# Scaling the features instead of the weights, with a new job order and a new block schedule, in a fused transformer block

## The chip, the cores and the metric

The kernel runs on one core of one Trainium2 chip. The metric is device microseconds (us) for one execution. A comparison is made with runs of the kernel before that were timed on the same chip in the same rounds; its medians in the four sets of rounds after the prediction lie between 392.31 and 392.51 us, so times of different sets may be compared to about 0.2 us. The span of a profile is about 2 us shorter than the time of the same execution, so profiles are compared with profiles and times with times.

The engines are called TensorE (PE; its weight loads PEld), VectorE (DVE), ScalarE (ACT), GpSimd (POOL) and SyncE (SP, which issues nearly all transfers).

## The reference

The reference is one block with modulation from a vector c: layer norm, attention with softmax feature maps (32 heads of 18 columns), a gated residual, layer norm, a two-layer network with ReLU, and a second gated residual.

```python
mod = (_silu(c) @ w_mod).reshape(c.shape[0], 6, 1, -1)      # sa, ca, ga, sb, cb, gb
h = _layernorm(x, axis=-1) * (1 + ca) + sa
x = x + ga * _A_ref(h, A_wqkv, A_w_phi, A_wo)
h = _layernorm(x, axis=-1) * (1 + cb) + sb
x = x + gb * _B_ref(h, B_w1, B_w2)
# _A_ref: q, k, v = h @ wqkv;  phi(u) = [softmax(u @ w_phi), softmax(-u @ w_phi)] per head
#         kv = phi(k)^T v;  o = phi(q) kv / (phi(q) z);  return o @ wo
```

There are 2048 rows of 576 columns (16 row tiles of 128) and 4608 hidden columns, all in bf16.

## The kernel before

It has two parts. The **front** does the attention statistics of all tiles, the queries, and the first two tiles up to the second norm. It is a list of jobs, written in a fixed order (ORDER); each engine gets its instructions in that order. A number after a job is a tile, and a number after a colon is a pair of PSUM banks. Then eight **feed-forward blocks** of two tiles follow. Each also carries, in hooks, the attention output, projection and norm of the two tiles that come next.

```python
ORDER = """
Z11 sx sd rp sc FK ca Z2 fs0 fsr frr fra2 sh frd4 fra0 fra1 bn1 fs3 bn0 fs1 Z1 fra3 shc sa0 wsd2 KR:0 fsd4 fs2
...
kv12 vE14 rK15 kv13 V15:1 qs1 pA15 gar pM15 kv14 Q2:2 vE15 qp1 kv15 eQ2 Q3:0 tp0 wo4 qt1 kz Q4:1 eQ3 wo2 sq2
...
"""
# Z: filler matmuls on zeros   sc, sh: products that give the modulation's scale and shift   FK: fold of w_k with w_phi
# fs, fsr, fsd, wsd, FQs: scaled weight copies   fra, frr, frd: unscaled ones (wfold)   KR, VR, QR: row corrections
# K, V, Q: projections of a tile   pM: GpSimd part of the key softmax   kv: K^T V product
# qs, qp, qt: query softmax (VectorE, GpSimd) and its DMA transpose   gar: the gate row's load   wo: wo *= gate row (GpSimd)
# ... cut ...
    def mods(w, outs, width, bank, idle=None):
        o = PS[:, bank, :] if isinstance(bank, int) else bank[:, 0, :]
        for k, wm in enumerate(w):
            for ci in range(NC):
                if idle is not None:
                    spin(1, idle)                       # one filler matmul of 512 columns
                for ck in range(NC):
                    pe.matmul(...)                      # one column each
# ... cut ...
        # the query softmax of a later tile q, as the hooks below do it:
        #   q_fin(q): q_sm on VectorE, q_pool on GpSimd, q_turn: DMA transpose; then q_in(q + NL), a reload, if there is one
        def in_l1(g, u):
            if (g, u) in ((0, -1), (0, 1)): ...         # the two query softmaxes
            if (g, u) in ((1, 2), (2, 1)):              # attention output of the two tiles, then its DMA transpose
                num_mm(t, pr); num_o(t, pr); turn_dma(oT[:, t % 2], o_sb[:, t % 2, :])
        def in_l2(pos):
            if pos in (1, 4): ...                       # projection wo_mm (5 chunks of 128 rows), residual, statistics
            if pos in (2, 6): ...                       # second norm, then its DMA transpose into h2
            if pos == 12:                               # scale and shift h2 for the next block
                for ci in range(NC):
                    dve.tensor_scalar(out=hb[:, ci, :], in0=hb[:, ci, :], scalar1=..., scalar2=..., op0=ALU.mult, op1=ALU.add)
```

The softmax here doesn't subtract the row's maximum and nothing guards it: scores larger than these inputs give would overflow.

Of the kernel before, what the change touches and what calls it, by code (L numbers as in the profile page):

```python
# [43 lines left out]
Z11 sx sd rp sc FK ca Z2 fs0 fsr frr fra2 sh frd4 fra0 fra1 bn1 fs3 bn0 fs1 Z1 fra3 shc sa0 wsd2 KR:0 fsd4 fs2  # L44
sp0 bn2 T0:2 VR:1 KRh bn3 Tc0 Ka0:2 KRd sa2 wsd1 sp2 VRh Kb0 wsd0 Ka1:0 wsd4 eKa0 VRd Kb1 wsd3 T2:1 eKa1 sK0
V0:2 Tc2 sK1 FQ3:0 rK0 K3:1 FQra3 pA0 FQs3 pM0 vE0 eK3 K2:0 bn4 bn5 rK1 kv0 eK2 FQ1:2 pA1 V1:1 sK3 pM1 FQra1
m2:0 vE1 rK3 sa4 pA3 sK2 FQs1 kv1 sp4 V2:1 m2c pM3 bn7 rK2 T4:2 V3:0 bn6 Tc4 pA2 vE2 pM2 sa6 K4:2 vE3 K5:1
bn10 eK4 sp6 bn9 T6:0 kv2 Tc6 kv3 eK5 sK4 ga:2 K7:0 gac sK5 rK4 K6:1 eK7 pA4 pM4 bn8 V4:2 eK6 sK7 gb:0 sa8
V5:1 vE4 wl0 rK7 sp8 rK5 sK6 pA7 T8:2 gbc kv4 pA5 Tc8 FQ2:0 pM5 K8:2 vE5 rK6 FQrd2 K9:1 bn11 eK8 w2a2 pA6 pM6
bn14 kv5 sa10 V6:2 FQs2 sK8 eK9 sp10 wl1 V7:0 pM7 vE6 rK8 sK9 T10:1 V8:2 Tc10 pA8 vE7 pM8 K10:1 rK9 vE8 w2a0  # L50
kv6 bn12 eK10 FQ0:0 pA9 FQ4:2 kv7 pM9 FQrd0 kv8 FQrd4 V9:1 FQs0 w2b0 bn13 FQs4 QR:0 vE9 K11:2 QRh sa12 QRe
sK10 sp12 kv9 eK11 V10:1 bn15 QRd wl4 rK10 T12:0 V11:2 sK11 Tc12 pA10 sa14 pM10 K13:0 gbw vE10 rK11 wl2 Q0:1
pA11 eK13 sp14 vE11 pM11 kv10 eQ0 T14:2 sK13 K12:0 w2a1 Tc14 qs0 kv11 rK13 K14:1 eK12 pA13 pM13 V13:2 eK14
sK12 wl3 K15:0 qp0 vE13 rK12 sK14 V12:1 eK15 pA12 pM12 qt0 Q1:2 vE12 rK14 sK15 gbr V14:0 pA14 eQ1 gaw pM14
kv12 vE14 rK15 kv13 V15:1 qs1 pA15 gar pM15 kv14 Q2:2 vE15 qp1 kv15 eQ2 Q3:0 tp0 wo4 qt1 kz Q4:1 eQ3 wo2 sq2
tp2 Q5:2 eQ4 sq3 tp1 wo3 nu0:3 eQ5 Q6:0 sq4 nO0 wo0 qi2 Q7:1 eQ6 wo1 sq5 ot0:2 w2b1 eQ7 nu1:3 Q8:0 nO1 oc0
Q9:1 eQ8 W0:3 eQ9 sq7 lb0 ot1:2 sq8 Q10:0 oc1 sq6 lr0 W1:1 ap0 eQ10 sq9 lb1 xc0 ht0:2 sq10 Q11:0 ha0 hd0 lr1
Q12:3 eQ11 ap1 Q13:2 qi3 xc1 eQ12 sq11 ht1:0 Q14:1 hd1 ha1 sq12 eQ13 Q15:3 qi4 eQ14 sq13 eQ15 sq14 sq15
# [3 lines left out]
def tile_block(ctx, tc, a, out):  # L62
# [42 lines left out]
    wv_raw = carve(R1, 12760, (NC, D))  # L105
    wfold = carve(R1, 15640, (NC, D))
# [96 lines left out]
    load(sp, flat(wsc), "wsc")  # L203
    load(sp, flat(wkT), "wkT")
    load_xT(0)
    load(sp, flat(wsh), "wsh")
    load_x(0, 2)
    load(sp, flat(wv_raw), "wv")
    load_x(2, 2)
    load_xT(1)  # L210
    load_x(4, 2)
    load(sp, epsr[:], "epsr")
    load(sp, flat(wqT), "wqT")
    load_xT(2)
# [28 lines left out]
    def mods(w, outs, width, bank, idle=None):  # L243

        o = PS[:, bank, :] if isinstance(bank, int) else bank[:, 0, :]
        for k, wm in enumerate(w):
            for ci in range(NC):
                if idle is not None:
                    spin(1, idle)
                for ck in range(NC):  # L250
                    pe.matmul(o[0:width, k * NC + ci:k * NC + ci + 1], lhsT=wm[0:R, ck, ci * width:(ci + 1) * width],
                              rhs=siluc[0:R, ck:ck + 1], start=(ck == 0), stop=(ck == NC - 1))
# [152 lines left out]
    def wo_mm(t, pr, add_x):  # L405
        for k in range(2):
            if add_x:
                pe.matmul(pr[:, k, 0:HD], lhsT=ident[:, 0:P], rhs=x_sb[:, t, k * HD:(k + 1) * HD], start=True, stop=False)
            for ci in range(NC):
                pe.matmul(pr[:, k, 0:HD], lhsT=oT[:, t % 2, ci, :], rhs=wo_sb[:, ci, k * HD:(k + 1) * HD],  # L410
                          start=(ci == 0 and not add_x), stop=(ci == NC - 1))
# [5 lines left out]
    def ln2_apply(t, src):  # L417
# [4 lines left out]
        if src is None:  # L422
            cols(xn[:, t % 2, 0:D], x_sb[:, t, :])
            cols(xn[:, t % 2, D:640], x_sb[:, t, 512:D])
        else:
            cols(v2(xn[:, t % 2, 0:D]), src[:, :, 0:HD])
            cols(xn[:, t % 2, D:640], src[:, 1, 224:HD])
# [15 lines left out]
    def f_scaled_d(dst, ck):  # L443
        dve.tensor_scalar(out=dst[0:R, ck, 0:G5], in0=PS[0:R, ck, 0:G5], scalar1=ca1[0:R, ck:ck + 1], scalar2=None, op0=ALU.mult)

    def f_scaled(dst, ck):
        act.activation(out=dst[0:R, ck, 0:G5], in_=PS[0:R, ck, 0:G5], func=ACT.Copy, scale=ca1[0:R, ck:ck + 1])

    def f_raw(eng, ck):
        if eng is act:  # L450
            act.activation(out=wfold[0:R, ck, 0:G5], in_=PS[0:R, ck, 0:G5], func=ACT.Copy)
        else:
            eng.tensor_copy(out=wfold[0:R, ck, 0:G5], in_=PS[0:R, ck, 0:G5])
# [12 lines left out]
    SS = RS[:, 0:6 * HD].bitcast(FP32).rearrange("p (a f) -> p a f", f=HD)  # L466
    X, Y, Z = 6, 4, 7
# [8 lines left out]
    def rows_h(pr):  # L476
        act.activation(out=v2(tmpr[X0:NX, :]), in_=pr[X0:NX, :, 0:HD], func=ACT.Copy)

    def rows_d(pr, dst):

        dve.scalar_tensor_tensor(out=v2(dst[X0:NX, 4, :]), in0=v2(tmpr[X0:NX, :]), scalar=mk[X0:NX, :],
                                 in1=pr[X0:NX, :, 0:HD], op0=ALU.mult, op1=ALU.add)
# [24 lines left out]

    def raw_copy(eng, o, i):
# [4 lines left out]

    def wv_scale(ck, eng):
        o, i, f = wv[0:R, ck, :], wv_raw[0:R, ck, :], ca1[0:R, ck:ck + 1]
        if eng is act:
            act.activation(out=o, in_=i, func=ACT.Copy, scale=f)
        else:
            eng.tensor_scalar(out=o, in0=i, scalar1=f, scalar2=None, op0=ALU.mult)

    def ln2_bn(i, pr):
        for hf in range(2):
            dve.bn_stats(out=st[:, i, hf, :], in_=pr[:, hf, 0:HD])
        dve.bn_aggr(out=mv[:, 1, i, :], in_=st[:, i])
# [71 lines left out]
    def k_minus(t):  # L596
# [7 lines left out]
    ROWS = {"K": wfold, "V": wv_raw, "Q": wfold}  # L604
    ROWD = {"K": wk, "V": wv, "Q": wq}
# [6 lines left out]
        "sc": lambda: mods([wsc], None, R, 7, idle=6),  # L612
        "sh": lambda: mods([wsh], None, R, 7, idle=6),
        "shc": lambda: dve.tensor_copy(m98[0:R, :, X0 + 3], PS[0:R, 7, 0:NC]),
        "FK": lambda: fold_all(wkT),
        "fs": lambda c: f_scaled(wk, c), "fsd": lambda c: f_scaled_d(wk, c),
        "frd": lambda c: f_raw(dve, c), "fra": lambda c: f_raw(act, c),
        "fsr": lambda: dve.tensor_tensor(out=wk[0:R, :, G5:D], in0=last,
                                         in1=ca1[0:R, :].unsqueeze(2).to_broadcast([R, NC, FW]), op=ALU.mult),
        "frr": lambda: dve.tensor_copy(out=wfold[0:R, :, G5:D], in_=last),  # L620
        "rp": lambda: pool.tensor_copy(rep[0:R], siluc[0:R, :].unsqueeze(2).to_broadcast([R, NC, 32])),
        "wsd": lambda c: wv_scale(c, dve), "wsa": lambda c: wv_scale(c, act), "wsp": lambda c: wv_scale(c, pool),
# [8 lines left out]
        "FQs": lambda c: act.activation(out=v2(wq[0:R, c, :]), in_=at["FQ", c][0:R, :, 0:HD], func=ACT.Copy, scale=ca1[0:R, c:c + 1]),  # L631
        "FQrd": lambda c: raw_copy(dve, v2(wfold[0:R, c, :]), at["FQ", c][0:R, :, 0:HD]),
        "FQra": lambda c: raw_copy(act, v2(wfold[0:R, c, :]), at["FQ", c][0:R, :, 0:HD]),
        "Q": lambda t: proj(at["Q", t], t, wq), "eQ": lambda t: exps(t, at["Q", t], EQ[:, SLOT[t], :]),
        "sq": q_out, "qi": q_in, "qs": q_sm, "qp": q_pool, "qt": q_turn,
        "m2": lambda: mods([wsb, wcb], None, P, at["m2", None]), "m2c": lambda: mod2_e(at["m2", None]),
# [6 lines left out]
        "W": lambda i: wo_mm(i, at["W", i], True), "lb": lambda i: ln2_bn(i, at["W", i]), "lr": ln2_rs,  # L643
        "xc": lambda i: act.activation(out=v2(x_sb[:, i, :]), in_=at["W", i][:, :, 0:HD], func=ACT.Copy),
        "ap": lambda i: ln2_apply(i, at["W", i]),
# [4 lines left out]
    for w in "KV":  # L650
        JOBS[w + "R"] = lambda w=w: rows_mm(ROWS[w], at[w + "R", None])
        JOBS[w + "Rh"] = lambda w=w: rows_h(at[w + "R", None])
        JOBS[w + "Rd"] = lambda w=w: rows_d(at[w + "R", None], ROWD[w])
    for i, w in enumerate("Q"):
# [3 lines left out]
        JOBS[w + "Rd"] = lambda w=w, i=i: quarter_rows(i, ROWD[w])  # L658
# [42 lines left out]
    def l1(b, hooks):  # L701
        hb = h2[:, b % 2]
        for g in range(3):
# [5 lines left out]
            for u in range(3):  # L709
                l1_rest(js[u], u, hb)  # L710
            for u in range(3):
# [19 lines left out]
    def l2(b, hooks):  # L731
# [31 lines left out]
        fin(t + 1, 1, Z, 2)  # L763
        prod(X, A22, T4, al)
# [7 lines left out]
        rows, z = slice(t * P, (t + 1) * P), yt[:, 1, :]  # L772
        sp.dma_start(outf[rows, 0:HD], x_sb[:, t, 0:HD])
        pool.tensor_tensor(out=z, in0=SS[:, 1, :], in1=gb_row[:, HD:D], op=ALU.mult)
        pool.tensor_tensor(out=z, in0=z, in1=x_sb[:, t, HD:D], op=ALU.add)
        prod(Z, A12, B22, al)
        dve.tensor_tensor(out=yt[:, 0, :], in0=PS[:, Z, 0:HD], in1=gb_row[:, HD:D], op=ALU.mult)
        dve.tensor_tensor(out=x_sb[:, t, HD:D], in0=yt[:, 0, :], in1=z, op=ALU.add)
        sp.dma_start(outf[rows, HD:D], x_sb[:, t, HD:D])

    NB = NT // 2
    for b in range(NB):
# [3 lines left out]
        def in_l1(g, u):  # L786
            if not more:
                return
            if (g, u) in ((0, -1), (0, 1)):
                q = t0 + max(u, 0)  # L790
                q_fin(q)
                if q + NL < NT:
                    q_in(q + NL)
            if (g, u) in ((1, 2), (2, 1)):
# [133 lines left out]
```

## Time and profile before

| what | kernel before | from |
|---|---|---|
| time | 393.02 us, median of 3 | runs before the prediction |
| span of the profile | 390.7 us | page |
| first feed-forward matmul | 93.52 us | timeline of TensorE |
| blocks 0 to 6 | 37.05 us each | starts of their first matmuls |
| last block, to the end | 37.83 us | same |
| TensorE busy | 98% | page |

The front and the blocks are read apart, because a change in one says nothing of the other. TensorE is the bound, so each question is whether something takes matmuls away or makes TensorE wait. The lines that show this stand in the prediction.

### The profile page before, as it was taken

How to read it: one execution, taken by the hardware profiler on the slowest of the kernel's cores; microseconds unless marked ns; L12 is line 12 of the kernel's file. 1: busy time of each engine (PE TensorE's matmuls, PEld its weight loads, DVE VectorE, ACT ScalarE, POOL GpSimd, SP SyncE). 2: the span in 40 equal slices, each digit the busy share in tenths (PEclk: the TensorE clock that was granted, in tenths of full speed). 3: DMA queues.
4: the chain of work that ended last, by engine and by line, in shares of the span. 5: the costliest groups of instructions: out<-in, count | busy, mean ns of one | idle time of the engine just before them, and what ended most of it. 6: DMA issues, size and time to landing. Idle time of an engine off the chain costs nothing.

```text
span 390.7 us, 8908 instructions
## 1 busy us (share of the span) xinstructions
PE 383.8 (98%) x3693; PEld 311.7 (80%) x3693; DVE 244.3 (63%) x452; ACT 157.9 (40%) x360; POOL 142.3 (36%) x199
## 2 busy tenths in 40 slices
PE   8999999999999999999999999999999999999995
PEld 4778888878887888788888878887888788878874
DVE  0889998854879746573755567458555664653221
ACT  1798779699531233124213510531143123312510
POOL 2155858741101510740164045306510641072045
PEclk9999999999999999999999999999999999999999
DMA  7999739795732151125313311450143124010001
GB/s 291 418 420 403 274 133 354 178 306 161 189 65 35 47 121 20 35 61 109 35 27 83 80 35 32 107 65 19 47 93 35 24 69 51 18 34 33 3 0 32
DMA packets 49515, 44.36 MB, mean 114 GB/s; under 512 B 39361, under 2 KB 42050, under 8 KB 48706
## 3 DMA queue, kind: packets, MB, share of 16 engines
q1 hardware_dynamic: 49186, 43.59, 39.6%
q8 instruction: 29, 0.48, 0.5%
q10 hardware_dynamic: 288, 0.19, 0.2%
q14 instruction: 12, 0.10, 0.1%
HBM read 27.97 MB, written 6.49 MB: 88 GB/s over the span
## 4 chain that ended last, share of the span: by engine, by line
PE 86%; POOL 6%; ACT 2%; DVE 2%; DMA 2%; issue 1%; SPq 0%; POOLq 0%; DVEq 0%; ACTq 0%
PE PS L683 33%; PE PS L742 29%; PE PS L274 9%; PE PS L410 5%; PE PS L690 5%; POOL wo_sb L637 2%; PE PS L235 2%; PE PS L391 1%; ACT RT L279 1%; POOL RH L754 1%; DMA gatd<-gt 1%; PE PS L324 1%; POOL RT L291 1%; DMA ga_row<-gatd 1%; DVE st L240 1%
## 5 line engine op out<-in xcount | busy, mean ns | idle before, releaser
L683 PE MATMUL PS<-h,R 128*128 128x256 bf16 x1152 | 133.5, 273 | 0.0
L683 PEld LDWEIGHTS <-R 128*128 128x128 bf16 x1152 | 109.8, 98 | 17.5 <-issue 5.1
L742 PEld LDWEIGHTS <-RH 128*128 128x128 f16 x864 | 84.5, 98 | 21.8
L728 POOL TENSOR_TENSOR yt<-yt,gb_row 128x288 f32<-128x288 f32 x23 | 16.8, 731 | 167.0 <-DVE yt L727 167.0
L742 PE MATMUL PS<-R,RH 128*128 128x288 bf16 (+1 forms) x576 | 75.6, 286 | 0.0
L697 ACT ACTIVATE RH<-PS 128x256 f16<-128x256 f32 x72 | 27.7, 384 | 114.0 <-PE PS L690 107.4
L699 DVE SCALAR_TENSOR_TENSOR RH<-PS,RH 128x256 f16<-128x256 f32 x72 | 30.1, 419 | 68.2 <-ACT RH L697 68.2
L279 ACT ACTIVATE RT<-PS,rs 128x576 bf16<-128x576 f32 x64 | 43.0, 750 | 7.5 <-PE PS L274 7.1
L698 ACT ACTIVATE RH<-PS 128x512 f16<-128x512 f32 x72 | 42.9, 595 | 7.8 <-PE PS L683 6.5
L746 ACT ACTIVATE RS<-PS 128x288 f32<-128x288 f32 x24 | 9.9, 411 | 75.9 <-PE PS L742 75.9
L742 PE MATMUL PS<-RT,RH 128*128 128x288 f16 x288 | 37.9, 286 | 0.0
L274 PE MATMUL PS<-RH,R 116*128 116x288 bf16 x240 | 31.8, 286 | 0.5 <-ACT RH L631 0.5
L754 POOL TENSOR_TENSOR RH<-RH,RT 128x2304 f16<-128x2304 f16 x7 | 31.8, 4548 | 0.0
L274 PE MATMUL PS<-RH,RT 116*128 116x288 bf16 x240 | 31.7, 286 | 0.0
L274 PEld LDWEIGHTS <-R 116*128 116x128 bf16 x240 | 22.9, 98 | 6.4 <-issue 0.7
L274 PEld LDWEIGHTS <-RT 116*128 116x128 bf16 x240 | 22.7, 98 | 5.5
L420 DVE TENSOR_SCALAR xn<-x_sb,mv,rs 128x576 bf16<-128x576 bf16 (+1 forms) x28 | 22.4, 842 | 7.3 <-ACT rs L415 7.3
L729 POOL TENSOR_TENSOR x_sb<-yt,x_sb 128x288 bf16<-128x288 f32 x31 | 22.8, 737 | 5.9 <-DVE yt L725 4.1
L240 DVE BATCH_NORM_STATS2 st<-x_sb 128x6 f32<-128x288 bf16 x60 | 24.2, 445 | 0.5
L410 PE MATMUL PS<-wo_sb,oT 128*128 128x288 bf16 x160 | 22.6, 286 | 0.2 <-POOL wo_sb L637 0.2
L284 DVE TENSOR_REDUCE Rk<-RT 128x64 f32<-128x1152 bf16 x16 | 21.2, 1332 | 1.4 <-ACT RT L279 1.4
L284 DVE TENSOR_REDUCE Rq<-RT 128x64 f32<-128x1152 bf16 x16 | 21.5, 1342 | 0.0
(115 smaller groups left out, 414.2 us busy)
## 6 DMA issues: line engine op xcount, KB each, us to landing
R<-in_w1a_dram SPq DMA_DIRECT2D x4, 1152.0 KB
eqd<-RT SPq DMA_DIRECT2D x14, 288.0 KB, 5.8
RT<-eqd SPq DMA_DIRECT2D x14, 288.0 KB, 2.7
R<-in_w2a_dram SPq DMA_DIRECT2D x3, 864.0 KB, 10.4
R<-in_w2b_dram SPq DMA_DIRECT2D x2, 1296.0 KB, 10.9
out_dram<-x_sb SPq DMA_DIRECT2D x15, 144.0 KB, 3.3
RT<-in_xT_dram SPq DMA_DIRECT2D x2, 640.0 KB
x_sb<-in_xk_dram SPq DMA_DIRECT2D x3, 288.0 KB
```

The source lines that it names most:

```text
L240: dve.bn_stats(out=s[:, hf, :], in_=x_sb[:, t, hf * HD:(hf + 1) * HD])
L274: pe.matmul(pr[:, k, 0:HD], lhsT=xt(t, ck), rhs=w[0:R, ck, k * HD:(k + 1) * HD], start=(ck == 0), stop=(ck == NC - 1))
L279: act.activation(out=E.rearrange("p (b h s e) -> p b h s e", b=2, s=2, e=DH)[:, :, :, s, :], in_=pr[:, :, 0:HD].rearrange("p b (h e) -> p ...
L284: dve.tensor_reduce(out=Rr, in_=E.rearrange("p (c e) -> p c e", e=DH), axis=AXX, op=ALU.add)
L410: pe.matmul(pr[:, k, 0:HD], lhsT=oT[:, t % 2, ci, :], rhs=wo_sb[:, ci, k * HD:(k + 1) * HD], start=(ci == 0 and not add_x), stop=(ci == NC ...
L683: pe.matmul(PS[:, 2 * u + hf, n * 256:n * 256 + 256], lhsT=w1a[:, ci, jj * P:(jj + 1) * P], rhs=hb[:, ci, :], start=(n == 0 and ci == 0), ...
L697: act.activation(out=A11[:, j, :], in_=lo[:, :, 0, :], func=ACT.Relu)
L698: act.activation(out=A2[:, j, :, :], in_=PS[:, 2 * u + 1, :].rearrange("p (n s f) -> p n s f", n=2, s=2), func=ACT.Relu)
L699: dve.scalar_tensor_tensor(out=U3[:, j, :], in0=lo[:, :, 1, :], scalar=0.0, in1=A11[:, j, :], op0=ALU.max, op1=ALU.subtract)
L729: pool.tensor_tensor(out=x_sb[:, t, c], in0=y, in1=x_sb[:, t, c], op=ALU.add)
L742: pe.matmul(PS[:, bank, 0:HD], lhsT=am[:, j, :], rhs=bm[:, j, :], start=first and j == 0, stop=(j % 9 == 8), skip_group_check=True)
L754: pool.tensor_tensor(out=A12, in0=A12, in1=U2, op=ALU.subtract)
```

## The change

The intent has five parts: scale the transposed features once and keep one copy of each weight; add the first two residuals on VectorE instead of by identity matmuls; do the half-filled fifth chunk of the output projection as two 64-row matmuls that run beside each other; split the last product in two; and take a new order for the front, searched under the assumption that all loads behind the first eight arrive later. Cut to its core:

```diff
-Z11 sx sd rp sc FK ca Z2 fs0 fsr frr fra2 sh frd4 fra0 fra1 bn1 ...
+Z11 sx sd rp sc bn1 Z2 bn0 FK ca sa0 sp0 fra0 frd4 sh fra1 frr fra2 xd0 T0:0 fra3 Z2 shc Tc0 Ka0:2 ...
 ... cut: the rest of the order; in it
+... QRe QRd V15:1 rK14 sK15 pA14 gar V12:2 pM14 vE14 rK15 Q0:0 vE12 pA15 wo1 vE15 kv12
+eQ0 Q1:2 pM15 Q2:1 qs0 eQ1 wo4 kv13 eQ2 kv14 qs1 kv15 qp0 Q3:0 sq2 tp0 Q4:2 qp1 ...
-    load_x(0, 2)                        # was behind wkT, xT0, wsh
+    load_x(0, 2)                        # now third
-                if idle is not None:
-                    spin(1, idle)
-        "sc": lambda: mods([wsc], None, R, 7, idle=6),
-        "sh": lambda: mods([wsh], None, R, 7, idle=6),
+        "sc": lambda: mods([wsc], R, 7),
+        "sh": lambda: mods([wsh], R, 7),
+    def x_scale(t, eng): ...             # xT of two tiles times (1 + ca); on VectorE, ScalarE or GpSimd
-            if add_x: pe.matmul(pr[:, k, 0:HD], lhsT=ident[:, 0:P], rhs=x_sb[...], start=True, stop=False)
+    def add_res(t, pr): dve.tensor_tensor(out=x, in0=x, in1=pr[:, :, 0:HD], op=ALU.add)
+    def wo_rest(t, pr):                  # fifth chunk: 64 rows at 0 and the same 64 rows at 64, one half of the columns each
+        for k in range(2): pe.matmul(pr[:, k, 0:HD], lhsT=oT[b0:b0 + 64, t % 2, 4, :], rhs=wo_sb[b0:b0 + 64, 4, ...], ...)
         def in_l1(g, u):
+            if b < 2:
+                ...                       # as before, and
+                if b and (g, u) == (1, 0): q_next(t0 + 2)
+                return
+            if (g, u) in ((0, 0), (0, 2)): attend(t0 + u // 2)
+            if g and u == "rest": wo_rest(t0 + g - 1, pair(3))
+            if g and u == 0: wo_full(t, pair(3)); add_res(t, pair(3)); bn(1, t)
+            if (g, u) == (1, 2): norm2(b, t0)
         def in_l2(pos):
 ... cut
+            if pos == (6 if b < 2 else 1): norm2(b, t0 + 1)
+            if b > 1 and pos in (4, 9) or b == 1 and pos == 9: q_next(t0 + 2 + pos // 9)
```

## The prediction

> **What bounds the kernel now.** I read the page's parts 1 and 2 first, then the table of stretches, then the chain in order of time, then TensorE's waits, last the timeline of the first 26 us and of the last 26.
>
> ```profile
> span 390.7 us, 8908 instructions
> PE 383.8 (98%) x3693; PEld 311.7 (80%) x3693; DVE 244.3 (63%) x452; ACT 157.9 (40%) x360; POOL 142.3 (36%) x199
> PE   8999999999999999999999999999999999999995
> ```
>
> TensorE is busy in every slice but the first and the last. Ends of matmuls are modelled, so I checked this with its waits. These are all there are before the feed-forward part begins at 93.68 us (us in total, times, longest):
>
> ```profile
> PE PS L235 <- POOL eps_t L227: 1.3, 1, 1.3
> PE PS L268 <- DVE RS L614: 0.7, 1, 0.7
> PE PS L274 <- ACT RH L631: 0.5, 1, 0.5
> PE PS L577 <- DVE RH L481: 0.3, 1, 0.3
> PE PS L410 <- POOL wo_sb L637: 0.2, 1, 0.2
> ```
>
> After the first 14 us only 1.0 us of waiting is left. So the time is matmul count times spacing, plus the start, plus the tail. The chain from 93.68 us on gives the spacing (start, length, what; the first of eight feed-forward blocks):
>
> ```profile
> 93.68 3.06 PE PS L683 x28
> 96.74 0.76 PE PS L690 x12
> ...
> 113.95 1.23 PE PS L410 x10
> ```
>
> 28 matmuls in 3.06 us: 109 ns for 256 columns. Ten L410 matmuls (288 columns, the output projection of one row tile) in 1.23 us: 123 ns each. Twelve L690 matmuls, which use only 64 rows of the array each, in 0.76 us: 127 ns a pair, little more than one full matmul. Blocks start at 93.68, 130.73, 167.78 and so on: 37.05 us each, seven times. VectorE is busy 22 of these 37 us, so it has room there. It has less in the front (length, PE, PEld, DVE, ACT, POOL busy with counts, clock, DMA share, GB/s):
>
> ```profile
> 0.00:13.25 13.25, 11.95 (x99) 7.40 (x99) 3.57 (x12) 5.24 (x9) 2.22 (x11) 1.00 0.84 323
> 13.25:93.68 80.43, 78.74 (x869) 64.21 (x869) 68.89 (x121) 65.98 (x152) 45.28 (x97) 1.00 0.82 292
> ```
>
> VectorE 68.9 and ScalarE 66.0 of 80.4 us: not the bound, but close behind.
>
> **What the Trainium skill says.** (1) "TensorEngine Tiling (Array Packing)", Key Properties: tiles of different rows can load and multiply in parallel, and changing the tiling mode drains the array. The trace agrees with the first: 127 ns a pair at L690 against 109 ns for one full matmul at L683. The 20 ns over may be the mode change; the trace doesn't separate it. (2) "TensorE: Matmul & The Clock Gate", What's actually happening: the array starts at half rate until about 3.4 us of activity. The trace agrees: the first 12 filler matmuls took 5.30 us (0.44 each), later ones stand about 0.22 us apart. So fillers keep the array awake, and cost nothing while data is awaited. (3) "SBUF — State Buffer", SBUF: two separate sides: VectorE with two SBUF inputs and GpSimd hold one port pair exclusively. The change gives GpSimd three long multiplications; the trace of before has none like them in the front, so it doesn't tell.
>
> **The change part by part.**
>
> *a. Fewer matmuls in blocks 2 to 6.* The fifth chunk of the output projection has only 64 real rows. Row tiles 6 to 15 now do it as two 64-row matmuls (one for each half of the columns) right behind the L690 ones, already in that mode, so no mode change is added. A tile has 8 full matmuls and one pair instead of 10: 10 x 123 ns becomes 8 x 123 + about 125, so 0.12 us less. Ten tiles: **-1.2 us**, all on the path, as TensorE has no gap there. Price: a 64-column copy on ScalarE before each transposing DMA (estimate 0.3 us each; ScalarE is busy 10.6 of 37 us), hidden. The attention steps move a stage earlier, which only lengthens the slack of the 2.6 and 3.2 us transposes.
>
> *b. No residual matmul in the front.* The four identity matmuls at L408 go: 4 x 0.123 = **-0.5 us**. The addition moves to VectorE, twice about 0.75 us (as L305, 128x576 from PSUM, 748 ns), while ScalarE loses two copies of 0.65. VectorE has four projections (4 x 1.23 us) in which to hide it.
>
> *c. Scaled features instead of scaled weights.* Removed from VectorE: five scalings of wv (1.7), two scaled fold copies (0.73 + 0.53); from ScalarE: four scaled fold copies (2.6) and five for wq (3.6). Added: ten 116x256 scalings on VectorE (estimate 0.25 each, from 366 ns for 576 columns), fifteen on ScalarE (estimate 0.38 each, from the 116x504 copy's 599 ns), three 116x1280 multiplications on GpSimd (estimate 2.6 each, from L291's 1,166 ns for 576). So VectorE and ScalarE come out within 1 us of where they were, GpSimd gains 7.8 us in the front, to 55 of 94. None of this is TensorE time. It counts only where TensorE waited: at the start.
>
> *d. The start.* Before, the first useful stream is the row correction at 14.16 us, after waiting 0.7 us for the shift copy, and the K projection follows at 16.74. Fillers: 24 before, 19 after. I walked the new order by hand, with landings read off when the load queue could go on: wsc about 6.3, wkT 7.9, xT0 8.7, wsh 10.4, x01 11.1, wv 13.1 us. With x01 moved to the third place they become about x01 7.0, wkT 8.7, wsh 10.4, xT0 11.1, x23 12. Then: scale matmuls end at 7.75; fold 8.75 (waits for wkT) to 10.2; shift to 11.85; four fold copies on ScalarE end at 11.9; VectorE's statistics, fold copies and first five scalings end at 12.5; K projection (four chunks) from 12.4; row correction 13.4; second K part to 15.6; fillers; its last chunk waits until 16.3 to 16.85 for the corrected rows; and V of tile 0 ends about 24.3. By then 14.2 us of useful matmuls are done since 6.3, so 3.8 are lost to waits and fillers. Before, the comparable point (25.84, with 14.7 of useful work since 6.39) had lost 4.8. So **-1.0 us**.
>
> *e. The tail.* The last product is cut into halves of 144 columns, and the addend prepared while TensorE runs. Before, two VectorE steps of 0.46 follow the last matmul, and the last store is issued at 387.98. Now the last two are half as wide (estimate 0.3 each): about **-0.3 us**. GpSimd has the two preparing steps before the other tile's residual, so that tile's 144 KB store leaves later, about 386.9, and takes 3.3: it can become the last, which is why I take no more.
>
> Sum: -1.2 - 0.5 - 1.0 - 0.3 = -3.0, so 390.0 from 393.02. The order was searched for exactly such waits, and an early load made safer is worth more than my walk sees: I shade to **389.8 us**, 0.8% less.
>
> **The rivals.**
> *R1: the front gains nothing or loses.* VectorE is busy 37.6 of the 40 us from 10 to 50, and the new order puts statistics, scalings and corrections in one queue ahead of the first K tile; the GpSimd multiplications could hold up the corrected keys (its L291 and L594 jobs gate the KV products) or hold VectorE's port. For: so little room there. Against: the total work of VectorE and ScalarE is unchanged, and TensorE hardly waited after 24 us. It would give 391 to 392.5.
> *R2: the start gains much more.* Without extra waits TensorE would go from 6.3 us straight through: all 3.8 us of lost time is the ceiling, and about half of it could be had if the loads land before my walk has them. Then 387 to 388.
> *R3: new waits in the blocks.* Attention moved into the first group makes ScalarE wait for VectorE's normalisation before the next relu; the pair of PSUM banks used for the projection is also the accumulator of the second layer. For: these are in-order queues. Against: the relu's bank is needed again only about 3 us later, and VectorE is 60% busy. It would give back the 1.2 us: 391.
> *R4: the loads.* Slots of the load queue free up in order; the new order delays wkT and xT0. If those are 2 us later than I think, the start loses its 1 us and one more: 391.5.
>
> **How the range and the chances follow.** Parts a and b are sure to 0.2 us (1.7 in all). Part d carries plus or minus 1.5, the tail 0.3, runs differ by 0.7. So 387.6 to 391.8 in 8 of 10. Faster by over 2% needs under 385.3: even R2 with everything else ends at 387. Slower by over 2% needs 7.9 us more, for which nothing in the trace speaks. So 0.03, 0.96, 0.01.
>
> **What would show each step right or wrong.** (a) Blocks 2 to 6 last 36.8 us, the first two 37.05; a new TensorE wait there on the projection banks or the transposed tile means R3. (b) No identity matmuls, and no wait of TensorE on normalised rows before 93 us. (c) VectorE's and ScalarE's sums up to the first feed-forward matmul within 2 us of 72.5 and 71.2, GpSimd near 55; scalings of about 0.25, 0.38 and 2.6 us. (d) First K matmul near 12.4 us rather than 16.7, the feed-forward start near 92.0 rather than 93.68; if it starts before 91, R2 holds, and if after 93, R1 or R4: the releaser of TensorE's waits between 10 and 40 us tells which (VectorE or GpSimd, or a DMA). (e) From the last matmul to the end 0.3 us less than before. The prediction is wrong if TensorE shows several us of waits in the front that these steps don't hold, or if the blocks changed by anything other than the packed pairs.

## The result and the profile after

The changed kernel takes 404.98 us (median of 4 runs, 404.75 to 405.16), against 392.51 us for the kernel before in the same rounds. The ratio is 1.0317, with a 95% interval of 1.0293 to 1.0341: the mean of one kernel's runs over the mean of the other's in the same rounds, so not quite the ratio of the medians. It is slower by 3.2%, where a gain of 0.8% was forecast.

From the page of the changed kernel: the span, TensorE's busy tenths and the granted clock in tenths, in 40 slices.

```profile
span 403.4 us, 8950 instructions
PE   7999999878999998999999999999999999999996
PEclk9599999999999999999999999999999999999999
```

Two things are new. TensorE is no longer full in slices 8 to 10 (70 to 100 us), and in the second slice the granted clock is half. TensorE's waits in the whole span (us in total, times, longest), of which the longest are:

```profile
PE PS L671 <- DVE h L857: 2.1, 5, 0.4
PE PS L270 <- ACT RT L275: 2.0, 2, 1.3
PE PS L387 <- DMA RE<-RT: 1.4, 2, 0.9
...
PE PS L404 <- DMA oT<-o_sb: 1.2, 1, 1.2
PE PS L320 <- POOL RT L287: 1.2, 1, 1.2
```

(The cut line is the wait at the very start, 1.3 us, which both kernels have.) Five different releasers appear; behind its start the kernel before waited 1.7 us in all. The places where the 12.7 us of span went:

| stretch | before | after | difference |
|---|---|---|---|
| first feed-forward matmul | 93.52 | 102.57 | +9.05 |
| block 0 | 37.05 | 37.05 | 0 |
| block 1 | 37.05 | 38.45 | +1.40 |
| blocks 2 to 6 | 185.25 | 187.42 | +2.17 |
| block 7 and tail | 37.83 | 37.88 | +0.05 |

**The start.** From the changed kernel's chain of work (start, length, what): the fold, the shift products, the first K part and the row correction.

```profile
8.62 2.80 PE PS L432 x25
11.42 2.44 PE PS L247 x25
...
15.01 1.92 PE PS L270 x8
16.93 2.18 PE PS L264 x10
```

Before, the 25 fold matmuls took 1.46 us and ten row-correction matmuls 1.23. Here they take nearly double: this is the half clock, in every matmul from 8.6 to about 19 us. The 25 scale products just before (from 6.07 us) had taken 1.49 us, which is the full rate, so the array was fast and became slow. The V projection of tile 0, the last step that the prediction walked through, ends at 28.22 us.

**The GpSimd queue.** GpSimd's timeline in the changed kernel (start, length, engine, line, operation, what, count, idle time before and who ended it), then that of the kernel before:

```profile
71.42 0.36 POOL L587 TENSOR_SCALAR Ak<-rk,rs 128x32 f32<-128x32 f32 x1
74.14 1.27 POOL L625 TENSOR_TENSOR wo_sb<-wo_sb,ga_row 128x576 bf16<-128x576 bf16 x1 [2.36 <-DMA ga_row<-gatd]
```

```profile
71.73 1.17 POOL L291 TENSOR_TENSOR RT<-RT,ratq 128x576 bf16<-128x576 bf16 x1
75.18 7.39 POOL L637 TENSOR_TENSOR wo_sb<-wo_sb,ga_row 128x576 bf16<-128x576 bf16 x5 [2.29 <-DMA ga_row<-gatd]
```

Both stand still for 2.3 us until the gate row has landed, at nearly the same time. Before, nothing was behind that wait but the wo scalings themselves: the keys and the first two query softmaxes were done. Now the last key softmax (at 75.87) and both query softmaxes (79.37 and 82.34) are behind it. Before, only one TensorE wait of 0.2 us came of it (on wo_sb); now the waits on POOL's RT and on the transfer RE<-RT listed above do (2.6 us as listed). Not all of GpSimd's delay is the gate row: from 78.2 to 82.3 us, beside a VectorE tensor_tensor of 4.45 us (L463), two of its ratio jobs take 1.07 us instead of 0.25 and one multiplication 1.86 instead of 1.17. What that part alone costs was not tested.

**The blocks.** At the end of block 2, VectorE's timeline in the changed kernel shows the five scalings of h2; below them is what GpSimd ran at that time.

```profile
214.08 2.84 DVE L857 TENSOR_SCALAR h<-h,mod 128x256 bf16<-128x256 bf16 x5
```

```profile
213.24 1.17 POOL L287 TENSOR_TENSOR RT<-RT,ratq 128x576 bf16<-128x576 bf16 x1
214.37 0.73 POOL L717 TENSOR_TENSOR yt<-yt,gb_row 128x288 f32<-128x288 f32 x1
215.17 1.41 POOL L718 TENSOR_TENSOR x_sb<-yt,x_sb 128x288 bf16<-128x288 f32 x2
```

In the kernel before the same five took 1.71 us at the corresponding place, beside a GpSimd with one short job (0.73 us):

```profile
203.40 1.71 DVE L820 TENSOR_SCALAR h<-h,mod 128x256 bf16<-128x256 bf16 x5 [0.21 <-DMA h<-xn]
```

They also start early enough now (about 1.7 us before TensorE ends the block, at about 215.8, against 1.4 before), so it is their length that makes TensorE wait. The listed wait of 0.4 us is too small, as it is counted from the modelled end of the matmul before: the third and fourth matmul of block 3 start 287 and 686 ns after the one ahead of them instead of 109, so 0.76 us is lost. The Trainium skill, "SBUF — State Buffer", Who interferes with whom, says that a VectorE tensor_scalar in a two-port mode and a GpSimd instruction each take a shared port pair whole and block the other. That would fit; the experiments test it.

In block 1 SyncE's queue shows why the transposed attention output comes late:

```profile
153.40 1.86 SPq L346 DMA_TRANSPOSE RE<-RT  x1
157.25 0.33 SPq L335 DMA_DIRECT2D RT<-eqd  x1
157.68 3.50 SPq L399 DMA_TRANSPOSE oT<-o_sb  x2
```

The first attention output was ready at 153.6 us (its VectorE instruction started at 152.81 and took 0.76). Its transpose was issued 4 us later, because a reload stood ahead of it in the queue that could go only once the third query softmax's transpose had read that buffer. TensorE then waited 1.2 us for it.

### The profile page after: what moved, and what is told of

The parts are those of the page before. It is cut to its first block, busy times and chain, and to the rows that moved or that the text cites. A ratio compares the mean times of both kernels' runs of the same rounds, so it can differ in the third digit from the quotient of the medians.

```text
span 403.4 us, 8950 instructions
## 1 busy us (share of the span) xinstructions
PE 387.7 (96%) x3701; PEld 313.5 (78%) x3702; DVE 238.0 (59%) x463; ACT 157.0 (39%) x376; POOL 147.3 (37%) x202
## 4 chain that ended last, share of the span: by engine, by line
PE 78%; DMA 7%; POOL 4%; DVE 4%; ACT 2%; issue 2%; SPq 1%; POOLq 0%; DVEq 0%; ACTq 0%
PE PS L671 31%; PE PS L731 23%; PE PS L270 9%; PE PS L678 5%; DVE h L857 3%; PE PS L804 3%; ACT RT L275 2%; DMA R<-in_wkT_dram 2%; PE PS L387 1%; DMA eqd<-RT 1%; PE PS L404 1%; POOL RH L743 1%; POOL RT L287 1%; DMA h<-xn 1%; PE PS L247 1%
## 5 line engine op out<-in xcount | busy, mean ns | idle before, releaser
L671 PEld LDWEIGHTS <-R 128*128 128x128 bf16 x1152 | 111.1, 98 | 18.8 <-issue 5.9
L731 PEld LDWEIGHTS <-RH 128*128 128x128 f16 x846 | 82.8, 98 | 20.8
L731 PE MATMUL PS<-R,RH 128*128 128x288 bf16 (+1 forms) x558 | 72.4, 286 | 0.0
L687 DVE SCALAR_TENSOR_TENSOR RH<-PS,RH 128x256 f16<-128x256 f32 x72 | 28.8, 413 | 62.7 <-ACT RH L685 62.7
L270 PE MATMUL PS<-RH,R 116*128 116x288 bf16 x240 | 32.9, 291 | 0.5 <-ACT R L573 0.5
L238 DVE BATCH_NORM_STATS2 st<-x_sb 128x6 f32<-128x288 bf16 x64 | 25.9, 447 | 3.8 <-DMA x_sb<-in_xk_dram 3.2
L716 DVE TENSOR_TENSOR yt<-PS,RS 128x288 f32<-128x288 f32 x23 | 10.4, 451 | 29.7 <-POOL RH L743 24.0
L409 DVE TENSOR_TENSOR x_sb<-x_sb,PS 128x576 bf16<-128x576 bf16 x16 | 12.0, 751 | 15.5 <-PE PS L804 8.1
```

Of the source, the lines that this page charges most:

```text
L238: dve.bn_stats(out=s[:, hf, :], in_=x_sb[:, t, hf * HD:(hf + 1) * HD])
L270: pe.matmul(pr[:, k, 0:HD], lhsT=xt(t, ck), rhs=w[0:R, ck, k * HD:(k + 1) * HD], start=(ck == 0), stop=(ck == NC - 1))
L671: pe.matmul(PS[:, 2 * u + hf, n * 256:n * 256 + 256], lhsT=w1a[:, ci, jj * P:(jj + 1) * P], rhs=hb[:, ci, :], start=(n == 0 and ci == 0), ...
L687: dve.scalar_tensor_tensor(out=U3[:, j, :], in0=lo[:, :, 1, :], scalar=0.0, in1=A11[:, j, :], op0=ALU.max, op1=ALU.subtract)
L731: pe.matmul(PS[:, bank, 0:HD], lhsT=am[:, j, :], rhs=bm[:, j, :], start=first and j == 0, stop=(j % 9 == 8), skip_group_check=True)
```

## The experiments

Twelve kernels ran, all correct. "Front" below is the start of the first feed-forward matmul in the profile.

### e1_idle: the fillers back

```diff
-        "sc": lambda: mods([wsc], R, 7),
-        "sh": lambda: mods([wsh], R, 7),
+        "sc": lambda: mods([wsc], R, 7, idle=6),      # and spin(1, idle) back in mods
+        "sh": lambda: mods([wsh], R, 7, idle=6),
```

> The changed kernel with the ten filler matmuls put back between the groups of the scale and shift products (one before each group of five). Theory C (the array went back to half rate because only one-column matmuls and waits ran from 6 to 11 us): the granted clock of the second fortieth is full again, the fold takes about 1.5 us instead of 2.80, the shift products with their fillers about 2.3, the first K part 1.0 instead of 1.92, the row correction 1.25 instead of 2.18; net of about 1.5 us for the fillers the point where V of tile 0 ends comes 2 to 3.5 us earlier, and the kernel takes about 402. Rival (the early stream is set by loads and by the fold copies, not by the clock): the clock is restored, but that point moves by less than 1 us and the time stays within 404.3 to 405.5.

Measured: 400.45 us (400.27 to 400.56), front at 98.94 us, 3.6 us earlier. The same stretch, from TensorE's timeline (fold, first K part, row correction):

```profile
9.21 1.56 PE L434 MATMUL PS<-RS,R 126*116 126x126 bf16 x25
...
13.46 1.15 PE L272 MATMUL PS<-RH,R 116*128 116x288 bf16 x8
14.44 1.39 PE L266 MATMUL PS<-RH,RS 116*100 116x288 bf16 x10
```

All are at the full rate, and although ten matmuls were added, the first K part starts 1.3 us earlier (13.46 against 14.80). Theory C holds: fewer instructions made a longer start. V of tile 0 ends at 24.95 us instead of 28.22. The other 0.9 us of the gain in time is not the clock's: blocks 1 and 2 were 1.0 us shorter in this execution (37.71 and 37.31 us), which no edit here explains.

### e2_wo: the two wo scalings behind the query softmaxes

```diff
-... vE12 pA15 wo1 vE15 kv12 eQ0 Q1:2 pM15 Q2:1 qs0 eQ1 wo4 kv13 ... Q4:2 qp1 eQ3
+... vE12 pA15 vE15 kv12 eQ0 Q1:2 pM15 Q2:1 qs0 eQ1 kv13 ... Q4:2 qp1 wo1 wo4 eQ3
```

> The changed kernel with the two early GpSimd jobs that scale wo chunks 1 and 4 by the gate row moved behind the two softmax jobs of the first query tiles, as the kernel before had them. Theory P (GpSimd's in-order queue stands 2.4 us waiting for the gate row's DMA and starves the key products and the first query transposes): TensorE's waits on L287 (1.16 us) and on the transposed RE (1.4 us) go, the feed-forward part starts 2 to 4 us earlier, time about 402. Rival (these waits come from the whole front being late, and the chain through the quarter rows and the gate row decides): the wait on GpSimd goes, another takes its place, feed-forward start within 1 us of 102.7, time 404 to 405.5.

Measured: 400.31 us (399.66 to 401.82), front at 96.79 us, 5.8 us earlier, more than I had expected. TensorE's waits on L287 and on the transposed RE are gone. But 1.5 us of the 5.8 are luck with the clock: V of tile 0, long before the edit, ends at 26.70 us instead of 28.22, because the array was slow for less long (fold 2.23 us against 2.80, row correction 1.40 against 2.38, both from the timeline). That leaves 4.3 us for the queue.

### e3_hooks: the block schedule of before

```diff
-            (the whole in_l1 and in_l2 of the changed kernel)
+            (those of the kernel before; the 64-column copy of o_sb goes as well)
```

> The changed kernel with the schedule of the kernel before in the eight feed-forward blocks (whole fifth chunk of the projection, attention in groups 1 and 2, projection and norm in the second layer, query softmax at the start of the first layer). Theory B (the new block schedule itself loses 3.6 us: block 1 1.9, block 2 0.9, blocks 3 to 5 0.4 each): all seven blocks are 37.05 us again and the time is about 401.4; the front stays at 102.7. Rival (the late front pushes its stores and loads into the first blocks, and these stalls come from there): block 1 still takes over 38 us, and the time is over 403.

Measured: 401.20 us (398.08 to 401.88). All seven blocks take 37.05 us in the profile, and the front stays at 102.29. Theory B holds: the block schedule's loss is its own and not the front's echo. (The run of 398.08 us stands apart; see the next experiment.)

### e4_h2act: the h2 scalings on ScalarE

```diff
-                    dve.tensor_scalar(out=hb[:, ci, :], in0=hb[:, ci, :], scalar1=..., scalar2=..., ...)
+                    act.activation(out=hb[:, ci, :], in_=hb[:, ci, :], func=ACT.Identity, scale=..., bias=...)
```

> The changed kernel with only the five scalings of h2 at the end of each block (L857) moved from VectorE to ScalarE. Theory S (GpSimd's query softmax and residual work, moved to the end of the block, holds the SBUF port pair that these VectorE instructions need: they take 2.84 us instead of 1.71): on ScalarE they take about 0.4 to 0.5 us each, untouched by GpSimd, TensorE's wait of 2.1 us on L857 goes, blocks 3 to 5 take about 36.85 instead of 37.46, time about 402.5 to 403. Rival (they are late because VectorE's queue is late or because the transposed rows land late): TensorE waits as long on the ScalarE version, blocks 3 to 5 stay at 37.4 to 37.5, time 404.5 or more.

Measured: 400.28 us (398.69 to 402.42). The five scalings take 0.59 us each on ScalarE, longer than on an undisturbed VectorE (0.33), but always the same (0.585 to 0.600). Blocks 3 to 6 take 36.71 us, shorter than in the kernel before, and 0.76 less than in the changed kernel: the loss that the starts of the matmuls gave, not the 0.4 of the listed wait. Block 1 still takes 38.17.

The wide range of this kernel and of e3 has a cause that this run shows by accident. Its page gives the full clock everywhere, and its first matmuls are slow all the same:

```profile
PEclk9999999999999999999999999999999999999999
```

```profile
9.34 2.75 PE L432 MATMUL PS<-RS,R 126*116 126x126 bf16 x25
...
15.48 2.10 PE L270 MATMUL PS<-RH,R 116*128 116x288 bf16 x8
```

Here the array never reached the full rate before 17 us, and the record does not show it. The Trainium skill, "TensorE: Matmul & The Clock Gate", What's actually happening, says that the window that decides on the rate runs freely, so where it falls differs from execution to execution. I take the two groups of times of this kernel (398.7 and 398.9; 401.7 and 402.4) for two outcomes of that. Only one run of each kernel has its profile kept, so for the others it is inferred from the times.

### c1_idle_wo: fillers and wo scalings together

> Fillers back and the two wo jobs moved later, together; blocks as in the changed kernel. If theories C (half rate, 3.6 us of the front by the first run) and P (GpSimd's queue, 5.8 us by the second) are separate losses one after the other, the feed-forward part starts at about 93.2 us (102.57 - 3.6 - 5.8), as in the kernel before (93.52), and the time is about 395.5 to 396. If both runs only removed the same lateness, it starts at 96 or later and the time is 398 or more.

The edit is that of e1_idle and e2_wo. Measured: 396.96 us (396.39 to 398.62), front at 94.99. The two causes are separate, and they add once the luck of e2_wo is taken out. The end of V of tile 0 parts the front: the clock acts before it, GpSimd's queue behind it (us, from the starts of matmuls):

| run | edit to the front | V of tile 0 ends | from there to the first feed-forward matmul |
|---|---|---|---|
| changed kernel | none | 28.22 | 74.35 |
| e1_idle | fillers | 24.95 | 73.99 |
| p1_qearly (below; full rate by chance) | none | 24.61 | 73.68 |
| e2_wo | wo jobs later | 26.70 | 70.09 |
| c1_idle_wo | both | 24.50 | 70.49 |

So the clock is worth 3.3 to 3.7 us and the queue 3.5 to 4.3, whichever is mended first. TensorE's waits on the late keys and on the first query transposes are gone, and 1.5 us of the front's loss remains.

### c2_best: ScalarE's scalings, and block 1's softmax later

```diff
-                if b and (g, u) == (1, 0):
+                if b and (g, u) == (2, 2):
                     q_next(t0 + 2)
```

> The last kernel with two more edits: the h2 scalings on ScalarE, and in block 1 the third query softmax moved from the start of group 1 to the end of group 2, behind both attention steps. Theory (block 1's 1.2 us wait on the transposed attention output comes from the third softmax and its transpose standing ahead of it in VectorE's, GpSimd's and SyncE's queues; the other blocks' loss is the port): block 1 takes about 37.05 us, blocks 2 to 6 36.7, feed-forward start about 93.2, so a time of 390.5 to 391.5, under the kernel before (392.4). Rival (block 1 is late for another reason): block 1 stays above 38 and the time is about 392.5.

Measured: 393.48 us (392.97 to 394.11), ratio 1.0028 (1.0013 to 1.0043). Block 1 takes 37.04 us: the third softmax in front of the attention steps was its cause. The time is 2 to 3 us above what I expected. The front stayed at 94.55, and blocks 3 and 4 took 36.87 and 37.63 us, because a reload (the same RT<-eqd) and the stores stood ahead of the attention transposes in SyncE's queue.

### c3_sc_only: fillers in the scale products alone

```diff
-        "sh": lambda: mods([wsh], R, 7, idle=6),
+        "sh": lambda: mods([wsh], R, 7),
```

> The last kernel with fillers only in the scale products (five), none in the shift products. It tells which idle stretch loses the clock. If the one before the fold (6 to 8.6 us, with the wait for wkT) decides, the clock stays full through the fold and the shift products run at full rate: five fillers (1.1 us) less before the first K part, so the same time as the last kernel or up to 1 us less. If one-column products alone let the clock drop, it drops during the shift products, the first K part and the row correction take 1.9 and 2.2 us, and the time is 1 to 3 us longer.

Measured: 394.71 us (393.78 to 395.33). In the profile the clock stays full: the 25 shift products take 1.49 us, and the first K part starts at 12.02 us, a full us before that of c2_best. That us is not kept. TensorE then waits 0.7 us for the load of wqT, and by 20.4 us it is where c2_best was (20.6). So five fillers were enough in this execution, and 25 shift products without fillers kept the full rate. That the stretch ahead of the fold decides is not shown by it: p1_qearly (below) kept the full rate with no filler at all, and b1_nofill lost it only after its shift products. What both c3 and p1 do show is that an earlier first K part (12.02 and 12.05 us, against 13.01 in c2_best) is gone by the end of V of tile 0 (24.52 and 24.61, against 24.50): past 13 us that stretch is paced by loads and copies rather than by TensorE. The time itself came out 1.2 us longer; in the profile blocks 1 to 4 had waits of up to 1.2 us each on transposes, so it does not speak on the fillers.

### b1_nofill: the kernel before without its fillers

```diff
-        "sc": lambda: mods([wsc], None, R, 7, idle=6),
-        "sh": lambda: mods([wsh], None, R, 7, idle=6),
+        "sc": lambda: mods([wsc], None, R, 7),
+        "sh": lambda: mods([wsh], None, R, 7),
```

> The kernel before with its ten fillers between the scale and shift products taken out, nothing else. Theory C says that their removal alone makes the start slower: the granted clock falls to half in the second fortieth in most runs, the row correction at 14.16 us comes 1 us later or takes 2.2 us instead of 1.25, and the time is 1.5 to 3.5 us longer than before (394 to 396). Rival (fillers are pure cost; the start waits for data): it is up to 1.5 us shorter or the same (391 to 392.5).

Measured: 393.32 us (393.08 to 394.90), ratio 1.0031 (1.0010 to 1.0053). Ten matmuls fewer make the kernel before slower too, by 1.0 us. The direction is that of theory C, the size below what I expected: in the profile only the first row correction ran at half rate (2.61 us for ten). The fillers are worth 1 us there and 3.6 us in the changed kernel. The fold ran at the full rate here (1.61 us, after a wait of 0.4 us for wkT), so the slow stretch began later and held less work. Why it began later was not tested.

### p1_qearly: GpSimd's softmax moved instead

```diff
             if (g, u) in ((0, 0), (0, 2)):
                 attend(t0 + u // 2)
+            if (g, u) in ((0, 1), (1, 1)):
+                q_next(t0 + 2 + g)
-            if b > 1 and pos in (4, 9) or b == 1 and pos == 9:
+            if b == 1 and pos == 9:
```

> The changed kernel with one edit: in blocks 2 to 6 the two query softmax steps (on VectorE and GpSimd) move from the second layer to the first, where GpSimd is idle for over 20 us; the h2 scalings stay on VectorE. Theory S (the port pair is held by GpSimd while the h2 scalings run): five L857 take about 1.7 us again instead of 2.84, TensorE's wait of 0.4 us a block goes, blocks 3 to 5 take about 36.8 to 36.9 instead of 37.47, block 1 stays at 38.5 and the front at 102.6; time about 402. Rival (VectorE with the five scalings at the block's end is too slow anyway, whoever runs beside it): L857 still takes over 2.5 us and blocks 3 to 5 stay at 37.4.

Measured: 402.63 us (398.56 to 403.29). VectorE's line at the end of block 2:

```profile
209.37 1.78 DVE L859 TENSOR_SCALAR h<-h,mod 128x256 bf16<-128x256 bf16 x5
```

With GpSimd's work elsewhere, the same five VectorE instructions take 1.78 us instead of 2.84, and blocks 3, 5 and 6 take 36.71 (block 4 had another wait for a transpose and took 37.81). Together with e4_h2act, theory S is shown from both sides: taking away either partner of the collision removes the loss in these blocks. That it is the port pair that they collide on is the skill's statement; the runs show that VectorE's scalings are slow while GpSimd works beside them. The profiled run took 398.56 us; the other three took 402 to 403. By chance it is also the cleanest evidence on the clock: with the front of the changed kernel, unedited and without fillers, the array stayed at the full rate (fold 1.61 us, mean granted clock 0.999 against 0.987 in the other three), V of tile 0 ended at 24.61 us and the front at 98.29.

### d2_blocks, d3_all, d4_blocks_tail: what is worth keeping

d2_blocks is the kernel before with only the mended block schedule. The last edit takes the reload out of the attention transposes' way:

```diff
-            q_next(t0 + 2 + pos // 9)
+            q_next(t0 + 2 + pos // 9, pos == 4)        # the second one's reload waits ...
                 attend(t0 + u // 2)
+                if u: q_load(t0 + 1)                   # ... for the next block's attention steps
```

d3_all is c2_best with that edit and with the tail's halves written to row 1 of yt, which GpSimd is not reading then. d4_blocks_tail is d2_blocks with that tail.

> The kernel before, front, weights and tail as they were, with the block schedule of the changed kernel mended: packed projection pairs, h2 scalings on ScalarE, block 1's third softmax at the end of group 2, and the reload of the second query issued behind the next block's attention steps, so that it can't stand ahead of the transposes in SyncE's queue. Theory (the packed pairs are worth about 0.3 us a block once the two new waits are gone): feed-forward start 93.5, blocks 0 and 1 37.05, blocks 2 to 6 36.72, so 1.7 us less than before: 390.7. Rival (the waits on the transposed attention output that the last kernels showed in blocks 3 and 4, 0.7 to 1.1 us, come back): blocks 2 to 6 vary between 36.7 and 37.9 and the time is 391.5 to 392.5.

> The changed kernel with everything mended: fillers back, wo jobs later, h2 scalings on ScalarE, block 1's softmax and the reload moved, and in the tail the last product's halves written to a buffer that GpSimd is not reading (yt row 1 instead of row 0). Expected: feed-forward start 94.5 to 95, as in the run without the last two edits, blocks 2 to 6 36.7 (1.0 us less), and 0.4 us less from the last matmul to the end: about 392.0. If the tail is bound by GpSimd's chain and the stores rather than by that buffer, it is 392.4.

> The second kernel of this batch with the changed kernel's split tail, with the buffer mended as in the third. Expected: 0.4 us less than the second kernel if the buffer was what took the tail's gain, so about 390.3; the same as the second if GpSimd's chain decides.

| run | time, us | ratio to before (95%) | front | blocks 2 to 6, each | last block to end |
|---|---|---|---|---|---|
| d2_blocks | 390.42 | 0.9955 (0.9943 to 0.9967) | 92.26 | 36.71 (block 3: 37.13) | 37.82 |
| d3_all | 392.88 | 1.0012 (0.9996 to 1.0029) | 95.66 | 36.71 to 36.75 | 37.61 |
| d4_blocks_tail | 390.57 | 0.9962 (0.9949 to 0.9975) | 92.97 | 36.72 (block 3: 37.19) | 37.64 |

d2_blocks beats both kernels, by 0.45% over the kernel before, whose median in these rounds was 392.36. Its blocks give 1.3 us of that in the profile; its front, which was not edited, happened to be 1.3 us earlier in this execution. (The same front starts the blocks at 93.52 us in the kernel before and at 92.97 in d4_blocks_tail, so a front varies by about that much.) What is left in block 3 of d2 and d4 is a listed wait of 0.2 to 0.3 us on a query transpose (RE<-RT). The mended tail is 0.2 to 0.3 us shorter in the profiles, but d4_blocks_tail is no faster than d2_blocks in time, so the tail is not shown to be worth anything. d3_all, with everything of the change mended, is only level with the kernel before: its front is still the slower one.

## Why the prediction was wrong

**The steps that failed.** There are three, and each stands in a sentence that took something to be free.

*Step d, the start.* "So fillers keep the array awake, and cost nothing while data is awaited" was borne out, but the walk then took all durations at the full rate although the change had removed those fillers. The walk itself was good: the fold starts at 8.62 us (walked: 8.75), and no later wait for a load is listed, so rival R4 is out, and V of tile 0, walked to "about 24.3", ends at 24.61 where this same front happened to run at the full rate (p1_qearly) and at 24.50 with the fillers back (c2_best). In the changed kernel it ended at 28.22: the half rate put 3.6 us on a term sized at -1.0. The prediction's sign for trouble here, the releaser of TensorE's waits between 10 and 40 us, could not show it: only 0.7 us of waits are listed there, because slow matmuls are not waits.

*Step c and the order.* "None of this is TensorE time. It counts only where TensorE waited: at the start." The engine sums came out as forecast: up to the first feed-forward matmul VectorE 72.5 us (within 2 us of 72.5), ScalarE 69.8 (71.2), GpSimd 55.5 (near 55). Scalings took 0.28, 0.49 and 2.32 us (estimates: 0.25, 0.38 and 2.6). What failed is the inference from sums to the path: I never read where the wo scalings stood in GpSimd's queue against the gate row's arrival. Two jobs moved ahead of a late load cost about 4 us (c1_idle_wo against e1_idle: 94.99 and 98.94). Rival R1 named GpSimd, but for its multiplications, and allowed it only 1 to 3 us.

*Step a, the blocks.* "The attention steps move a stage earlier, which only lengthens the slack" and "all on the path, as TensorE has no gap there". The packed pairs did pay: undisturbed blocks take 36.71 us instead of 37.05, so 0.34 us each, a little more than the 0.24 forecast. But moving the softmaxes and transposes to make room brought two losses: the h2 scalings beside GpSimd, 0.76 us a block (37.05 - 0.34 + 0.76 = 37.47), and SyncE's queue in block 1. Point 3 of the skill part named the port, but asked only about the front and about VectorE instructions with two inputs; these have one. Together, less the pairs' gain, the losses are 3.6 us (e3_hooks). Rival R3 gave this place, with a smaller sum (giving back 1.2) and other causes.

**What was right.** The pairs add no mode change. In the changed kernel's chain the pair and the eight full matmuls follow straight on the 64-row ones:

```profile
189.01 0.76 PE PS L678 x12
189.77 0.12 PE PS L798 x2
189.89 1.08 PE PS L804 x8
```

The pair takes 0.12 us. Eight full matmuls at 123 ns should take 0.98; I take the 0.10 over it for the change of mode, which before lay in the matmuls of the first layer (20 of them behind 64-row ones take 2.29 us in the chain, and 20 at 109 ns would be 2.18). Part b, the four identity matmuls, is gone, with one wait of 0.3 us near their place (the transposes of the normalised rows wait for ScalarE), but was not measured alone. Part e, the tail, gave nothing: GpSimd ran the preparing steps ahead of the other residual, and the buffer yt row 0 was still being read, so VectorE began on the first half only when the second product had ended too.

**The sum.** Of the 12.7 us of span, the clock is 3.6, GpSimd's queue 4.0, the block schedule 3.6; 1.5 of the front is left. It stays in all four mended kernels (front 94.55 to 95.66; the old front starts the blocks at 92.26 to 93.52). Here is the stretch up to the first feed-forward matmul, in the kernel before from the prediction's comparable point (25.84) and in c2_best from the end of V of tile 0 (length, then busy us and count of PE, PEld, DVE, ACT, POOL, the clock, the DMA share and GB/s):

```profile
25.84:93.52 67.68, 67.49 (x772) 55.33 (x771) 56.58 (x94) 55.23 (x128) 41.39 (x85) 1.00 0.78 268
```

```profile
24.50:94.55 70.05, 68.38 (x772) 55.30 (x771) 56.92 (x95) 56.59 (x135) 47.23 (x89) 1.00 0.77 276
```

The count of matmuls is the same, and so, within 0.1 us, is their work (an estimate from the spacing of each kind in the two traces). TensorE idles 1.7 us instead of 0.2, mostly behind ScalarE's query exponentials; the 0.9 us by which it is busy longer I take for waits hidden by modelled ends, as in the blocks. So even mended, the new order is 1.3 us ahead at this point and loses 2.4 us behind it. Which part of the new order does that, and whether scaling features instead of weights could pay in the old order, was not tried and stays open.

## What to carry to other kernels

Before taking filler matmuls out, look at the durations of the matmuls that come after them, and in more than one execution: the shorter stream may run at half rate, in some executions or in all. When jobs are reordered, look in each in-order queue, SyncE's too, for what now stands behind a job that waits for a late transfer; the engines' busy sums do not show it. And when work is moved to an idle engine's gap, check what runs beside it at that moment, since each can slow the other when they overlap (five VectorE scalings 2.84 us instead of 1.71; a GpSimd ratio job 1.07 instead of 0.25). A wait that is counted from a modelled end can be too small (0.4 us listed, 0.76 lost): compare the starts.

## What the Trainium skill lacked or had wrong

- "TensorE: Matmul & The Clock Gate", HAM oscillation: it speaks of idle gaps of over 3.4 us, and the section behind it of short idle times between groups, without a size. Here no gap of TensorE between its first fillers and the fold was longer than 0.6 us; the stream was 25 one-column matmuls, two fillers and a 0.6 us wait, and the array was at half rate from 8.6 us on (fold 2.80 us instead of 1.46). Of five profiled executions of this front without fillers four ran slow and one did not (p1_qearly); with one filler of 512 columns ahead of every five one-column matmuls none of four did (e1_idle, c1_idle_wo, c2_best, d3_all). No page says how sparse a stream may be and keep the clock, and these runs do not part the one-column matmuls from the waits.
- The same page, Seeing it yourself, warns that clock events in profiles can be unreliable. In e4_h2act the granted clock reads full in every slice while the fold takes 2.75 us. The first 12 fillers of the kernel before take 5.30 us, 0.44 each against 0.22 later, under a full reading.
- "TensorEngine Tiling (Array Packing)", Key Properties, says that a change of tiling mode drains the array but gives no cost: here it is 0.10 to 0.11 us by the differences above.
- "SBUF — State Buffer", Who interferes with whom, has the contention of VectorE and GpSimd. The size here: 128x256 tensor_scalar instructions take 0.33 us undisturbed and up to 0.89 beside GpSimd; five of them 2.84 us instead of 1.71.
- No page was found to say what a blocked reload costs the transposes behind it in SyncE's queue: in block 1 it was 4 us between the ready output and the issue of its transpose.
